# Reordering the start of a sparse-attention and feed-forward kernel: the order of chunk 0's head, and the places of chunk 1's attention steps

## The chip, the cores and the metric

The kernel runs on one NeuronCore of a Trainium2 chip. The core has five engines with queues of their own: TensorE (PE in the profile, with its weight loads as PEld), VectorE (DVE), ScalarE (ACT), GpSimd (POOL) and SyncE (SP, which here only issues DMAs). Each engine takes its instructions strictly in the order of the program, and engines meet through semaphores. The metric is the time of one execution on the device in microseconds, as the median of several runs; less is better.

## The reference

Attention over local and block-summary keys, followed by a gated two-layer network. Four batches, eight heads, 768 positions, head size 64; the network goes from 512 to 2048 and back.

```python
block, window = (32, 16)
k_sum = k.reshape(B, H, nb, block, D).max(axis=3)      # 24 summary keys
v_sum = v.reshape(B, H, nb, block, D).mean(axis=3)     # 24 summary values
scores_l = scale * q @ k.T ; masked where |i - j| >= window
scores_s = scale * q @ k_sum.T + log(block)
a = softmax(concat(scores_l, scores_s))
x = (a @ concat(v, v_sum))            # -> (3072, 512), heads side by side
h = x @ w_in
g = h * sigmoid(beta * h)
out = g @ w_out
```

Inputs and the output are float32; the kernel computes its matmuls in bfloat16.

## The kernel before

**Chunks.** A batch (768 rows of x) is a chunk; four chunks follow each other. A chunk has two parts on PE: the *h stage* (x times w_in, `h_tile`, `h_two`, `h_half`, with silu on ScalarE into `h_sb`) and the *o stage* (h times w_out, `o_mm`, in 24 "atoms" of four matmuls, four atoms to a block of 128 output rows; each block is copied to `o_sb` and stored by SP). The attention of chunk n+1 is spread over the stages of chunk n: `run(main, sides)` writes main step i and then every side step whose position is below i+1. So a position such as 4.5 means "after atom 4". Chunk 0 has nothing to hide behind: its attention is the *head*, written out by hand from line 565 on.

**Attention of a chunk.** The eight heads are four pairs g; a pair's two heads lie on the two halves of the 128 partitions.
- Keys: `kt0(g, bg, cp, km)` turns the loaded rows on PE into PSUM tile big[bg] (`turned`, L260), and `cp` copies them to kT[g] (ScalarE by `act_cp`, VectorE by `dve_cp`). `key_max_nat` (L237) takes block maxima into km[g]. Later chunks: `kt1` or transposing DMAs into kT, `windows_perm` to kw, `key_max_win` (L233), and `key_sums` on GpSimd (L241).
- Queries: `qt_pe` turns pair g in the head, `qt1` all pairs in chunk 1 (L276); copies go to qn[g].
- Scores: `scores0(g, u, bg)` (head) and `scores(b, g, u, bg)` compute half u of pair g into big[bg]; `weigh` takes the exponential on ScalarE (L335). In the head, half u=1 of pairs 2 and 3 is masked by VectorE later (`mask_e`, L339, with the tile `mask`); the other blocks of the head add `off` and `edge` on PE instead. In later chunks all are masked.
- Values: `load_v0`/`load_v` bring float32 values (`vst`), `v_cast` (L344) makes bfloat16 `ve`, `v_odd` (L351, L352) or two DMAs (`v_odd_dma`, L355, L356) make `vo`, the same shifted by 64 rows. Block sums: `vm0`, `vm0s` or `vm_all` on PE, copied to `vm_one` or `vm_sb`; `vm_rest` and `spread` put them into ve and vo.
- AV: `av0` (first half, `av_split`), `av_two` and `av_mm`; `norm` divides on VectorE (L440, L441) into `xn`.
- x turned: `x_pe` and `x_two` on PE in the head, `x_dma` later: a transposing DMA issued by ScalarE (L466) into xT, which the h stage reads.

PSUM has three double tiles big0 to big2 and two single ones, one0 and one1, which everything shares; a step that writes one waits for whoever still reads it.

**Loads.** GpSimd issues keys and queries of chunks 0 and 1 and the weights, w_in in four pieces, then w_out, chunk 1's keys, the rest of w_out and chunk 1's queries (`more_loads`). The first w_in load is held by `behind` until one exponential of the head is done. SP issues the values (those of chunk 1 wait for the last w_out piece), the `vo` DMAs, the stores of the output and, from chunk 2 on, keys (`key_load`, into `kst`) and queries. `blank_run(n)` puts n matmuls on zeros into PE's queue.

**Places of chunk 1's attention.** They stand at lines 704 to 723, over the 24 atoms of chunk 0's o stage: queries at 2.5, value casts at 2.88 to 3.55, scores at 4.5, 9 and 12, block sums at 9, AV at 12.12 for pair 0 and 16.1 to 16.3 for the others, and the loads of chunk 2's keys at 6.5.

Of the kernel before, what the change touches and what calls it, by code (L numbers as in the profile page):

```python
# [11 lines left out]
def kernel(  # L12
# [163 lines left out]
    select(band[:], 2 * W - 1, [[1, QT]], -1)  # L176
    select(As, -W, [[P, J6 + 1], [-block, nb]], 1)
    select(As, block - 1 + W, [[-P, J6 + 1], [block, nb]], -1)

    def more_masks():  # L180
        nc.vector.tensor_copy(out=mask[:], in_=band[:, None, :].to_broadcast([P, NT, QT]))
        nc.vector.memset(mask[0:W, 0], 0.0)
        nc.vector.memset(mask[NK:NK + nb], 1.0)

    def clear_kw():
        for g in range(G):
# [49 lines left out]
    def key_max_nat(g):  # L236
        nc.vector.tensor_reduce(out=km[g][:, NK:NK + nb], in_=kT[g][:, W:W + S].rearrange("p (n f) -> p n f", f=block),  # L237
                                op=ALU.max, axis=AX.X)
# [323 lines left out]
    def blank_run(n, w=P):  # L562
        warm(n, one[1][:, 0, 0:w])

    blank_run(30)
    load_beta()
    blank_run(32, QT)
    kt0(0, 0, act_cp)
    more_masks()
    blank_run(12, QT)  # L570
    kt0(1, 1, act_cp, False)
    blank_run(8)
    kt0(2, 2, dve_cp, False)
    key_max_nat(1)
    blank_run(10)
    kt0(3, 0, act_cp, False)
    blank_run(4)
    v_cast(nc.gpsimd, 0)
    v_odd(nc.gpsimd, 0, 0, 3)
    v_odd(nc.gpsimd, 0, 3, 6)  # L580
    select(mask[0:NK, NT - 1], QT + W - 1, [[0, QT]], -1)

    def av0(g, t):
        av_split(g, t[:, 0])
        norm(0, g, t, [0])

    qt_pe(0, 0, 1, act_cp)
    vm0(0, one[0], dve_cp)
    blank_run(9)
    vm_rest(nc.gpsimd, 0)  # L590
    qt_pe(0, 1, 2, dve_cp)
    scores0(0, 0, 0)
    scores0(1, 0, 1)
    key_max_nat(2)
    key_max_nat(3)
    we = scores0(0, 1, 2)
    av0(0, one[1])
    scores0(1, 1, 0)
    qt_pe(0, 2, 1, dve_cp)
    behind(load_w_in(0, 512), we)  # L600
    v_cast(nc.gpsimd, 1)
    x_pe(0, 0, 0, dve_cp, one[0])
    qt_pe(0, 3, 2, act_cp)
    scores0(2, 0, 0)
    v_odd(nc.gpsimd, 1, 0, 3)
    v_cast(nc.vector, 2)
    v_odd(nc.vector, 2, 0, 3)
    scores0(3, 0, 1)
    scores0(2, 1, 2, False)
    vm0s(1, 2, one[1], dve_cp)  # L610
    scores0(3, 1, 0, False)
    load_w_in(512, 1024)
    v_cast(nc.gpsimd, 3)
    av0(1, one[0])
    av_two(0, 1, [big[2][:, 0:1]])
    v_odd(nc.gpsimd, 3, 0, 3)
    vm0(3, big[1][:, 1:2], dve_cp)
    av0(2, one[1])
    x_pe(0, 1, 0, act_cp, one[0])
    av0(3, big[1][:, 0:1])  # L620
    load_w_in(1024, 1536)
    load_w_in(1536, 2048)

    def begin(p, lo, hi):
        for i in (2 * p, 2 * p + 1):
            h_begin(i, big[(2, 0, 1)[p % 3]][:, i % 2], lo, hi)

    begin(0, 0, 1)
    begin(1, 0, 1)
    x_pe(0, 2, 0, act_cp, one[1])  # L630
    silu_table()
    begin(0, 1, 2)
    begin(1, 1, 2)
# [44 lines left out]
    HB = [one[1], big[1], one[0]]  # L678
    run([lambda i=i: h_half(i, 1, HB[i % 3][:, 0]) for i in range(k2)], s)

    def load_keys(n):
        for g in range(G):
            key_load(n, g)


    def av_at(b, s, pos, bufs):
        for g in range(G):
            def av(g=g):
# [8 lines left out]
    def x_pe2(b, g, t):  # L697
        t = t.bitcast(bf16)[:, 0, 0:S]
        x = xn[(b, g)]
        for j in range(J6):  # L700
# [10 lines left out]
    for j, (g, u, bg, pos, late) in enumerate([(0, 0, 2, 4.5, 4.6), (0, 1, 1, 4.5, 4.61), (1, 0, 0, 4.5, 4.62), (1, 1, 2, 9, 9.2),  # L711
                                               (2, 0, 1, 9, 9.11), (2, 1, 0, 9, 9.12), (3, 0, 2, 12, 12.13), (3, 1, 1, 12, 12.14)]):
# [12 lines left out]

# [82 lines left out]
```

## Time and profile before

| what | us |
|---|---|
| three runs | 214.63, 215.19, 217.09 (median 215.19) |
| the profiled execution | 216.31, of which the span from first to last instruction is 214.5 |
| head: PE's first h matmul (L495) | starts at 24.31 |
| chunk 0's first o matmul (L527) | starts at 48.95 |
| chunk 1's first scores (L328) | start at 55.36, after 0.35 of waiting |
| chunk 1's block sums (L388) | start at 60.41 |
| chunk 1's first h matmuls (L509) | two at 76.08, the rest from 77.78 |
| chunks 2 and 3: h stage starts | 123.55 and 169.48 |

The granted TensorE clock is full (1.000) over the whole span. The page's 40 slices show where each engine and the DMA engines are busy, in tenths, 5.4 us to a slice:

```profile
PE   7989999999999979999999999999999999999993
PEld 7877666665445446665555466654555566654452
DVE  5497757299657723950798325744787200002121
ACT  2468595686767007778633046778450086650000
POOL 7938980002701103563003004444000000000000
PEclk9999999999999999999999999999999999999999
DMA  6999999999669999999689879999535500001212
```

A busy slice of PE need not be useful work: in the head, 105 of its matmuls are blanks. VectorE's row shows the two crowded stretches, slices 2 and 3 (5 to 11 us: 4 and 9) and slices 8 to 10 (43 to 59 us). The DMA row is at nine or more until 54 us: weights, keys, queries and values of chunk 1 come in one unbroken stream.

The transposing DMAs into xT before chunk 1's h stage took 4.9 to 6.8 us from issue to landing; over all twelve in the run the median is 4.0.

### The profile page before, as it was taken

Reading aid. Unit: us, or ns where it says so; the run is one execution under the profiler, and the core shown is the slowest. Engines: PE = TensorE matmul, PEld = TensorE weight load, DVE = VectorE, ACT = ScalarE, POOL = GpSimd, SP = SyncE. Lnnn points to the kernel's source line nnn. Section 1 sums busy time; section 2 is a strip of 40 time slices with the busy share of each in tenths; the row PEclk is TensorE's granted clock in tenths of the full one; section 3 lists DMA queues with packets and bytes.
Section 4 is the critical chain, followed back from the end, with each engine's and each line's share of the span. In section 5 each row is a group of like instructions: output and inputs, shape, how many; then the busy total and the mean of one; then the engine's idle time right before and its main releaser. Section 6 shows DMA issues by size and latency. Waiting matters only on the chain.

```text
span 214.5 us, 5288 instructions
## 1 busy us (share of the span) xinstructions
PE 205.0 (96%) x2225; PEld 122.0 (57%) x2242; DVE 109.4 (51%) x252; ACT 106.5 (50%) x140; POOL 54.2 (25%) x85
## 2 busy tenths in 40 slices
PE   7989999999999979999999999999999999999993
PEld 7877666665445446665555466654555566654452
DVE  5497757299657723950798325744787200002121
ACT  2468595686767007778633046778450086650000
POOL 7938980002701103563003004444000000000000
PEclk9999999999999999999999999999999999999999
DMA  6999999999669999999689879999535500001212
GB/s 122 197 224 170 192 180 206 206 207 216 132 191 229 222 239 228 221 201 167 135 256 229 188 167 232 165 206 201 133 124 111 151 11 0 0 3 49 98 49 98
DMA packets 74534, 34.08 MB, mean 159 GB/s; under 512 B 61440, under 2 KB 70032, under 8 KB 74512
## 3 DMA queue, kind: packets, MB, share of 16 engines
q1 hardware_dynamic: 57440, 24.05, 53.0%
q0 software_dynamic: 7440, 7.34, 21.4%
q10 hardware_dynamic: 9632, 2.37, 8.0%
q8 instruction: 17, 0.28, 0.6%
q14 instruction: 5, 0.04, 0.1%
HBM read 27.37 MB, written 6.29 MB: 157 GB/s over the span
## 4 chain that ended last, share of the span: by engine, by line
PE 82%; DVE 12%; DMA 3%; issue 2%; ACT 0%; DVEq 0%
PE one L527 34%; PE big L509 29%; PE big L495 5%; DMA xT<-xn 3%; DVE kw L247 2%; PE big L328 2%; PE one L544 2%; PE big L414 2%; DVE qn L247 2%; DVE km L233 2%; DVE w_out_sb L216 2%; DVE xn L441 1%; PE one L501 1%; DVE km L237 1%; PE big L315 1%
## 5 line engine op out<-in xcount | busy, mean ns | idle before, releaser
L527 PE MATMUL one<-w_out_sb,h_sb 128*128 128x512 bf16 (+1 forms) x383 | 83.4, 370 | 1.9 <-issue 1.4
L522 ACT ACTIVATE h_sb<-big,beta_sb 128x768 bf16<-128x768 f32 x48 | 42.7, 900 | 49.1 <-PE big L509 49.1
L509 PE MATMUL big<-xT,w_in_sb 128*128 128x384 bf16 x384 | 63.1, 326 | 1.2 <-DMA xT<-xn 1.2
L527 PEld LDWEIGHTS <-h_sb 128*128 128x128 bf16 x400 | 38.1, 98 | 41.3 <-issue 0.2
L509 PEld LDWEIGHTS <-w_in_sb 128*128 128x128 bf16 x384 | 37.6, 98 | 26.5 <-issue 1.4
L247 DVE COPY o_sb<-one 128x512 f32<-128x512 f32 x19 | 13.1, 690 | 45.1 <-PE one L527 44.9
L335 ACT ACTIVATE e<-big,bias 128x768 bf16<-128x768 f32 x32 | 26.7, 897 | 16.5 <-PE big L328 13.9
L339 DVE TENSOR_TENSOR e<-e,mask 128x768 bf16<-128x768 bf16 x26 | 14.3, 571 | 15.8 <-ACT e L335 15.7
L247 DVE COPY kw<-kT 128x960 bf16<-128x960 bf16 (+1 forms) x16 | 10.5, 696 | 15.1 <-DMA kT<-kn 14.9
L344 POOL CAST ve<-vst 128x832 bf16<-128x832 f32 x15 | 13.7, 926 | 6.9 <-DMA vst<-in_v_dram 3.8
L475 POOL CAST qn<-qst 128x768 bf16<-128x768 f32 x8 | 6.6, 826 | 32.7 <-DMA qst<-in_q_dram 32.7
L241 POOL COPY kw<-km 128x288 bf16<-128x288 bf16 x12 | 7.5, 633 | 26.6 <-DVE km L233 26.6
L441 DVE TENSOR_TENSOR xn<-big,r 128x768 bf16<-128x768 f32 (+1 forms) x14 | 12.6, 900 | 0.5
L495 PE MATMUL big<-xT,w_in_sb 128*128 128x384 bf16 x64 | 11.4, 326 | 0.0
L233 DVE TENSOR_REDUCE km<-kw 128x24 bf16<-128x768 bf16 x12 | 11.2, 946 | 0.2
L483 POOL CAST kn<-kst 96x1024 bf16<-96x1024 f32 x4 | 4.1, 1037 | 23.3 <-DVE e L339 22.8
L642 ACT ACTIVATE h_sb<-big,beta_sb 128x384 bf16<-128x384 f32 x16 | 8.1, 579 | 2.7 <-PE big L495 2.7
L544 PE MATMUL one<-blank 128*128 128x128 bf16 (+1 forms) x105 | 8.2, 249 | 1.3 <-DVE blank L125 1.3
L501 PEld LDWEIGHTS <-w_in_sb 128*128 128x128 bf16 x64 | 6.2, 98 | 4.1
L501 PE MATMUL one<-xT,w_in_sb 128*128 128x384 bf16 x44 | 8.1, 326 | 0.0
L544 PEld LDWEIGHTS <-blank 128*128 128x128 bf16 x105 | 7.0, 121 | 1.7 <-DVE blank L125 1.3
L495 PEld LDWEIGHTS <-w_in_sb 128*128 128x128 bf16 x64 | 5.9, 98 | 3.5
(126 smaller groups left out, 186.9 us busy)
## 6 DMA issues: line engine op xcount, KB each, us to landing
out_dram<-o_sb SPq DMA_DIRECT2D x23, 256.0 KB, 2.7
vst<-in_v_dram SPq DMA_DIRECT2D x13, 336.0 KB, 4.5
kst<-in_k_dram SPq DMA_DIRECT2D x8, 384.0 KB, 5.9
qst<-in_q_dram SPq DMA_DIRECT2D x8, 384.0 KB, 4.2
w_in_sb<-in_moe_w_in_dram POOLq DMA_DIRECT2D x4, 512.0 KB, 6.3
w_out_sb<-in_moe_w_out_dram POOLq DMA_DIRECT2D x4, 512.0 KB, 13.6
vo<-ve SPq DMA_DIRECT2D x12, 107.2 KB, 2.3
vst<-in_v_dram SPq DMA_DIRECT2D x3, 416.0 KB, 7.1
```

What stands on the lines that cost most here:

```text
L233: nc.vector.tensor_reduce(out=km[g][:, NK:NK + nb].rearrange("p (m n) -> p m n", n=2), in_=kw[g][:, :, W:W + QT].rearrange("p m (n f) -> p ...
L247: nc.vector.tensor_copy(out=o, in_=i)
L335: return nc.scalar.activation(out=e[:], in_=s[:, :, 0:HS], func=ACTF.Exp, bias=bias[:, 0:1], scale=scale)
L339: return nc.vector.tensor_mul(out=e.rearrange("p h (m q) -> p h m q", q=QT), in0=e.rearrange("p h (m q) -> p h m q", q=QT), in1=mask[:, No ...
L344: eng.tensor_copy(out=ve[:, g, lo:hi, 0:D], in_=vst[g][:, lo:hi])
L441: nc.vector.tensor_mul(out=x[:, 3 * us[0]:3 * us[0] + 3 * n].rearrange("p (k j) h d -> p k (j h) d", k=n), in0=tv[:, :, :, 0:D], in1=r[:, ...
L495: nc.tensor.matmul(t[:, 0:HS], w_in_sb[:, ki, i * P:(i + 1) * P], xT[:, ki, 0:HS], start=(ki == 0), stop=(ki == k1 - 1))
L501: nc.tensor.matmul(t[:, 0:HS], w_in_sb[:, ki, i * P:(i + 1) * P], xT[:, ki, lo:lo + HS], start=(ki == 0), stop=(ki == k1 - 1))
L509: nc.tensor.matmul(t[:, kk, 0:HS], w_in_sb[:, ki, i * P:(i + 1) * P], xT[:, ki, kk * HS:(kk + 1) * HS], start=(ki == 0), stop=(ki == k1 - 1))
L522: nc.scalar.activation(out=h_sb[:, i, :].rearrange("p (k m) -> p k m", k=2), in_=t[:, :, 0:HS], func=ACTF.Silu, scale=beta_sb[:, i:i + 1])
L527: nc.tensor.matmul(t[:, 0:hi - lo], h_sb[:, n, ms * P:(ms + 1) * P], w_out_sb[:, n, lo:hi], start=(n == 0), stop=(n == k2 - 1))
L544: nc.tensor.matmul(t, blank[:, 0:P], blank[:, 0:t.shape[-1]], start=True, stop=True)
```

## The change

Four things are rearranged; no arithmetic changes, and outside the head and chunk 1's attention nothing is touched.

- *Head, keys and masks.* The function `more_masks` (fill the whole `mask` tile from `band`, 128 partitions) is dropped. A memset of the summary rows (partitions 96 to 127) stands early, and the copy of the other 96 partitions, its small memset and GpSimd's select on the last tile come much later. Pair 1's block maxima follow its key copy at once; pair 3's keys are copied by VectorE instead of ScalarE. Four blank matmuls go, and nine become seven.
- *Head, order of pairs.* Both score halves of pair 0 come before pair 1's queries are turned, AV of pair 0's first half before pair 1's scores. The first w_in load is held behind pair 1's first exponential instead of pair 0's second (each the third that ScalarE takes). Pair 3's queries are turned ahead of x of pair 0.
- *Head, values.* Pair 2's cast goes from VectorE to GpSimd, right behind pair 1's; pair 1's odd part goes from GpSimd to VectorE. Block sums of pairs 1 and 2 come after all scores. AV of pair 3 and the turn of pair 2's x come ahead of the first h matmuls; pair 3's block sums are copied by ScalarE.
- *Chunk 1.* Scores, block sums, AV, x DMAs and table loads from atom 8 on are placed one atom earlier. The block maxima of pair 3 go from position 0.4 to 3.44, behind the query copies. Two of chunk 2's four key loads go from 6.5 to 2.896, the others to 3.56.

```diff
-    def more_masks():
-        nc.vector.tensor_copy(out=mask[:], in_=band[:, None, :].to_broadcast([P, NT, QT]))
-        nc.vector.memset(mask[0:W, 0], 0.0)
-        nc.vector.memset(mask[NK:NK + nb], 1.0)
...
     load_beta()
+    nc.vector.memset(mask[NK:P], 1.0)
     blank_run(32, QT)
     kt0(0, 0, act_cp)
-    more_masks()
     blank_run(12, QT)
-    kt0(1, 1, act_cp, False)
+    kt0(1, 1, act_cp)
     blank_run(8)
     kt0(2, 2, dve_cp, False)
-    key_max_nat(1)
     blank_run(10)
-    kt0(3, 0, act_cp, False)
-    blank_run(4)
+    kt0(3, 0, dve_cp, False)
...
-    select(mask[0:NK, NT - 1], QT + W - 1, [[0, QT]], -1)
...
     vm0(0, one[0], dve_cp)
-    blank_run(9)
     vm_rest(nc.gpsimd, 0)
-    qt_pe(0, 1, 2, dve_cp)
-    scores0(0, 0, 0)
-    scores0(1, 0, 1)
+    blank_run(7)
+    scores0(0, 0, 2)
     key_max_nat(2)
+    scores0(0, 1, 0)
+    qt_pe(0, 1, 1, dve_cp)
+    av0(0, one[1])
     key_max_nat(3)
-    we = scores0(0, 1, 2)
-    av0(0, one[1])
+    we = scores0(1, 0, 2)
+    behind(load_w_in(0, 512), we)
+    v_cast(nc.gpsimd, 1)
     scores0(1, 1, 0)
     qt_pe(0, 2, 1, dve_cp)
-    behind(load_w_in(0, 512), we)
-    v_cast(nc.gpsimd, 1)
+    qt_pe(0, 3, 2, act_cp)
     x_pe(0, 0, 0, dve_cp, one[0])
-    qt_pe(0, 3, 2, act_cp)
+    nc.vector.tensor_copy(out=mask[0:NK], in_=band[0:NK, None, :].to_broadcast([NK, NT, QT]))
+    nc.vector.memset(mask[0:W, 0], 0.0)
+    v_odd(nc.vector, 1, 0, 3)
+    v_cast(nc.gpsimd, 2)
     scores0(2, 0, 0)
-    v_odd(nc.gpsimd, 1, 0, 3)
-    v_cast(nc.vector, 2)
-    v_odd(nc.vector, 2, 0, 3)
     scores0(3, 0, 1)
     scores0(2, 1, 2, False)
-    vm0s(1, 2, one[1], dve_cp)
     scores0(3, 1, 0, False)
+    v_odd(nc.vector, 2, 0, 3)
     load_w_in(512, 1024)
     v_cast(nc.gpsimd, 3)
-    av0(1, one[0])
-    av_two(0, 1, [big[2][:, 0:1]])
     v_odd(nc.gpsimd, 3, 0, 3)
-    vm0(3, big[1][:, 1:2], dve_cp)
+    vm0s(1, 2, one[1], dve_cp)
+    av_two(0, 1, [one[0]])
+    av0(1, big[1][:, 0:1])
     av0(2, one[1])
-    x_pe(0, 1, 0, act_cp, one[0])
-    av0(3, big[1][:, 0:1])
     load_w_in(1024, 1536)
     load_w_in(1536, 2048)
+    select(mask[0:NK, NT - 1], QT + W - 1, [[0, QT]], -1)
+    vm0(3, big[2][:, 0:1], act_cp)
+    x_pe(0, 1, 0, act_cp, one[0])
...
+    av0(3, big[1][:, 0:1])
+    x_pe(0, 2, 0, act_cp, one[1])
     begin(0, 0, 1)
     begin(1, 0, 1)
-    x_pe(0, 2, 0, act_cp, one[1])
...
-         (.3, lambda: km_pe(2, nc.gpsimd)), (.4, lambda: km_pe(3, nc.gpsimd))]
+         (.3, lambda: km_pe(2, nc.gpsimd)), (3.44, lambda: km_pe(3, nc.gpsimd))]
...
-  (0, 0, 2, 4.5, 4.6), (0, 1, 1, 4.5, 4.61), (1, 0, 0, 4.5, 4.62), (1, 1, 2, 9, 9.2),
-  (2, 0, 1, 9, 9.11), (2, 1, 0, 9, 9.12), (3, 0, 2, 12, 12.13), (3, 1, 1, 12, 12.14)
+  (0, 0, 2, 4.5, 4.6), (0, 1, 1, 4.5, 4.61), (1, 0, 0, 4.5, 4.62), (1, 1, 2, 8, 8.2),
+  (2, 0, 1, 8, 8.21), (2, 1, 0, 8, 8.22), (3, 0, 2, 11, 11.13), (3, 1, 1, 11, 11.14)
...
-    s.append((12.09, silu_table))
-    s.append((9.0, lambda: vm_all(one[1], [dve_cp] * 4)))
-    s.append((9.05, lambda: spread(0)))
-    s.append((9.06, lambda: spread(1)))
-    av_at(1, s, [12.12, 16.1, 16.2, 16.3], [0, 1, 2, 0])
+    s.append((11.09, silu_table))
+    s.append((8.0, lambda: vm_all(one[1], [dve_cp] * 4)))
+    s.append((8.1, lambda: spread(0)))
+    s.append((8.11, lambda: spread(1)))
+    av_at(1, s, [11.12, 15.1, 15.2, 15.3], [0, 1, 2, 0])
     for g in range(G):
-        s.append(((12.2, 16.35, 16.4, 16.5)[g], lambda g=g: x_dma(1, g)))
-    s.append((6.5, lambda: load_keys(2)))
+        s.append(((11.2, 15.35, 15.4, 15.5)[g], lambda g=g: x_dma(1, g)))
+    for g in range(G):
+        s.append(((2.896, 2.897, 3.56, 3.561)[g], lambda g=g: key_load(2, g)))
```

More of the change, by code (lines that the diff above doesn't have):

```diff
@@ L679 @@
     run([lambda i=i: h_half(i, 1, HB[i % 3][:, 0]) for i in range(k2)], s)
-    def load_keys(n):
-        for g in range(G):
-            key_load(n, g)
     def av_at(b, s, pos, bufs):
@@ L710 @@
         s.append(((2.885, 2.895, 3.45, 3.55)[g], lambda g=g: v_odd_dma(g)))
-    for j, (g, u, bg, pos, late) in enumerate([(0, 0, 2, 4.5, 4.6), (0, 1, 1, 4.5, 4.61), (1, 0, 0, 4.5, 4.62), (1, 1, 2, 9, 9.2),
-                                               (2, 0, 1, 9, 9.11), (2, 1, 0, 9, 9.12), (3, 0, 2, 12, 12.13), (3, 1, 1, 12, 12.14)]):
+    for j, (g, u, bg, pos, late) in enumerate([(0, 0, 2, 4.5, 4.6), (0, 1, 1, 4.5, 4.61), (1, 0, 0, 4.5, 4.62), (1, 1, 2, 8, 8.2),
+                                               (2, 0, 1, 8, 8.21), (2, 1, 0, 8, 8.22), (3, 0, 2, 11, 11.13), (3, 1, 1, 11, 11.14)]):
         s.append((pos + .01 * j, lambda g=g, u=u, bg=bg: scores(1, g, u, bg)))
         s.append((late, lambda g=g, u=u: last_mask.update({1: mask_e(1, g, u)})))
-    s.append((12.09, silu_table))
-    s.append((9.0, lambda: vm_all(one[1], [dve_cp] * 4)))
-    s.append((9.05, lambda: spread(0)))
-    s.append((9.06, lambda: spread(1)))
-    av_at(1, s, [12.12, 16.1, 16.2, 16.3], [0, 1, 2, 0])
+    s.append((11.09, silu_table))
[3 more added lines that the diff above has]
+    av_at(1, s, [11.12, 15.1, 15.2, 15.3], [0, 1, 2, 0])
     for g in range(G):
-        s.append(((12.2, 16.35, 16.4, 16.5)[g], lambda g=g: x_dma(1, g)))
-    s.append((6.5, lambda: load_keys(2)))
+        s.append(((11.2, 15.35, 15.4, 15.5)[g], lambda g=g: x_dma(1, g)))
+    for g in range(G):
+        s.append(((2.896, 2.897, 3.56, 3.561)[g], lambda g=g: key_load(2, g)))
     run(main, s)
```

## The prediction

> **What bounds the kernel now.** I read the page's busy times first, then the chain of waits in order of time, then the list of waits, and last each engine's timeline from 0 to 82 us.
>
> ```profile
> PE 205.0 (96%) x2225; PEld 122.0 (57%) x2242; DVE 109.4 (51%) x252; ACT 106.5 (50%) x140; POOL 54.2 (25%) x85
> ```
>
> PE is busy for 205.0 of 214.5 us, so 9.5 us are open. The chain says where they lie; its columns are start, length, what.
>
> ```profile
> 7.95 0.95 DVE km L237
> 8.90 0.67 DVE mask L181
> 9.57 0.05 issue
> 9.62 0.09 DVE mask L182
> 9.71 0.20 issue
> 9.91 0.70 DVE mask L183
> 10.60 0.03 issue
> 10.63 0.96 DVE kT L247
> 11.59 0.86 DVE km L237
> 12.45 0.03 issue
> 12.48 0.30 DVE vm_one L247
> 12.78 0.03 issue
> 12.81 0.97 DVE qn L247
> ...
> 53.48 1.74 DVE qn L247 x2
> 55.22 0.14 issue
> ...
> 72.30 5.44 DMA xT<-xn
> 77.74 0.04 issue
> 77.78 20.64 PE big L509 x126
> ```
>
> The list of waits has what PE lost at these places (total, times, longest, in us):
>
> ```profile
> PE big L509 <- DMA xT<-xn: 1.2, 1, 1.2
> ...
> PE big L307 <- DVE qn L247: 1.0, 2, 0.6
> ...
> PE big L328 <- DVE qn L247: 0.3, 1, 0.3
> ```
>
> So three stretches set the end. In the head (to 24.3 us) VectorE's queue does; PE's "busy" there is mostly blank matmuls. At 55.2 PE waits for VectorE's query copies, at 77.8 for a transposing DMA. From 24.3 to 55 and from 77.8 to the end PE runs without a gap worth naming: an instant won on PE before those stretches is won at the end, if transfers keep up.
>
> **The change, part by part. Head.** I follow each engine's order after the change with the durations of before. ScalarE's first two kT copies end at 7.95 and 8.83 as now. VectorE: km0 7.95 to 8.90; the mask work of 1.70 us (8.90 to 10.60) leaves this place; km1 to 9.80 (0.9); kT2 to 10.75 (0.96); kT3, new here (ScalarE had it, 10.17 to 10.97), +0.9 to 11.65; vm_one +0.3 to 12.0; km2 +0.95 to 12.95. The memset that remains (0.70 for 24 partitions, now 32) starts near 5.35, where VectorE idles 2.59 us; uncovered it would cost those 0.70.
>
> PE: four blanks (0.33 us) go, so pair 0's query turn starts at 10.06 instead of 10.39. Its load is no bar: the value load ordered behind it issued at 9.91. ScalarE, rid of kT3, copies qn0 10.63 to 11.43 (0.80). Block sums of pair 0 10.52 to 11.02, seven blanks (0.067 each) to 11.49: covered by that copy. Pair 0's scores 11.50 and 12.11 (0.61 each), first exponential 12.32 (0.82 after its scores start, as now) to 13.22; now it starts at 13.24. Pair 1's query turn 12.74 to 13.20, then its copy on VectorE, 13.31 to 14.27, which is 0.5 later than now (12.81); under it PE does pair 0's AV (0.60) to 13.87 and waits 0.44. Pair 1's scores 14.31 to 15.53, where now the fourth scores block ends at 16.5. VectorE meanwhile normalises (0.2 and 0.56) and does km3, to 15.85. Query turn of pair 2 15.55; pair 3's needs exponential 3 (15.13 to 16.03), 16.07 to 16.53. qn2 on VectorE 16.12 to 17.08 (now 17.11 to 18.07), qn3 on ScalarE to 17.65. Pair 2's scores start at 17.12 instead of 18.12; the four exponentials end at 21.2 instead of 22.2.
>
> The tail. VectorE takes xT0 to 17.35, the mask copy (0.67) and memset to 18.1, both halves of the odd values of pair 1 (0.25 each) to 18.65, of pair 2 to 19.5: it would idle there (0.67 before vm_one now). GpSimd: the first w_in load waits for exponential 3, as now for the third one: issue 16.33 (now 16.63); casts of pairs 1 and 2 to 18.95 (0.88 each), w_in to 19.7, cast 3 to 20.6, its odd part to 21.7, two w_in loads to 23.3, the select to 23.55; then nothing has moved (its next copy started at 23.62). PE: block sums of pairs 1 and 2 at 19.30; AV of pair 0's second half 19.8; AV 1 at 20.25 after vm_one; AV 2 20.9; block sums 3 21.5 to 22.0, copied by ScalarE to 22.4 (bounded by 0.30 on VectorE's row and 0.48 on ScalarE's xT row; 0.3 taken, the nearer shape); AV 3 22.47 to 23.1; turn of pair 2 to 23.27; four h matmuls each (0.65) to 24.57. Here pair 3's turn starts, which now starts at 25.79 with the same work behind it: **1.22 us**. Bounds: qn1 could be 0.3 earlier, km3 or a cast 0.4 later, so 0.8 to 1.5.
>
> Do loads keep up? First w_in chunk lands 5.6 after 16.63, 22.2, need 23.27. The second lands at 25.8, need 26.05; the third at 28.3, need 28.7. Keys of chunk 1 land at 38.2 (27.6 plus 10.6), need 38.90; queries at 50.1 (30.59 plus 19.5), need 50.41. All hold, narrowly, with nothing issued later than now.
>
> **First chunk.** km3 (0.86) goes behind the two query copies. PE's turns end at 51.96 with the head's shift, so the copies run 52.0 to 53.74 and the scores start at 53.88 instead of 55.36: 1.48, of which 1.22 is the head's: **0.26**. The third wait (0.35) falls to 0.1. km3 now follows at 54.6 and its GpSimd copy (0.43) sits ahead of the last value cast; that cast waits for data until 56.8 anyway, so this costs nothing; if data came early, 0.43 on the cast.
>
> All scores, block sums and AV one atom sooner (4 matmuls, 0.87 us): PE's work is the same, only its order changes, so nothing is won on PE itself. AV of pairs 1 to 3, the normalisations and the transposes start 0.87 sooner against the h stage, whose wait is 1.21: **0.87**, up to 1.21 if the transposes land faster. ScalarE's output copy of row block 2 (0.59) now stands right before the last two exponentials, whose row starts 0.2 behind PE: 0.3 later, covered by VectorE's idle 1.08 before the normalisation at 69.41.
>
> Two key loads (384 KB each, 0.45 to 0.59 of SP's queue) move ahead of the first output store and the odd-value transfers of pairs 2 and 3. Waiting behind them on SP: vo2, vo3 (before 59.21 and 60.49, landing 2.1 later), and for those VectorE's spreading of pairs 2 and 3, at 64.00 now, 61.65 after. vo3 issues at 59.4 to 60.4 and lands 2.1 to 3.2 later (the two rows of vo landings, alone and beside value loads): 61.5 to 63.6, a wait of 0 to 1.9 against the idle 1.08. I take 0. In return the transposes no longer share engines with key loads that took 4.1 to 7.5 us from 61.65: they landed in 4.9 to 6.8 us here, 4.0 in the median of all twelve. That is up to 0.34 more; I take 0.05.
>
> Sum: 1.22 + 0.26 + 0.87 + 0.05 = 2.4 us. The profiled execution took 216.31 us (span 214.5 and 1.8 around it), so 213.9; it lies 1.12 above the median of the three runs, and from that median, 215.19, the time is **212.8 us**.
>
> **The rivals.** (a) *Value casts late, 15%.* PE now reaches chunk 1's block sums at 58.06 (60.41 less 1.48 and 0.87). The last cast ended at 57.98 after a wait for its load. Now vo0 and vo1 can go 0.9 sooner, beside that load; beside loads vo1 took 3.2 us against 2.1. If the load loses those 0.9, PE stands 0.9: gain 1.5, 213.7.
>
> (b) *Mask copy against a GpSimd cast, 7%.* The mask copy (17.35) would fall on the cast of pair 1 (17.14 to 18.0). If one had to wait for the other, casts end 0.67 later: block sums of pairs 1 and 2 0.35 later, and everything that GpSimd issues behind slips 0.67, which leaves the last cast of chunk 1 0.2 short: gain 1.85, 213.3. Against it: the copy ran at 8.81 for 0.75 us beside the cast at 8.47, which took 0.88, as the undisturbed one at 55.57. For it: the cast at 56.82 took 1.16 beside a mask multiply. [...]
>
> (c) *The key loads stand in the way, 10%, and slower 4%.* Between 46 and 58 us SP's issues took up to 2.07 each (the 48 KB value parts) and 1.71 (vo1). If the two key loads cost that, vo3 lands by 66 and the spreading waits 4.4, of which 3.3 reach the transposes. It decides from a wait of 1.08; from 3.4 the change is slower than before, at 4.4 by 0.9: 216.1; a third such issue makes it over 1%, 218.2. Against: four key loads in a row took 2.07 in all. At the mild end, 0.7 over the slack, 213.5. [...]
>
> (d) *The head's gain does not arrive, 8%*: a link of the long head chain is later than reckoned, or queries of chunk 1 (0.3 us of room) come late. Only the atom and the query copies remain: gain 1.2, 214.0.
>
> **The numbers.** Forecast 56%, its own range 212.2 to 213.2. Over 1% (2.15 us, about what a measurement of this kernel can tell from no change) faster means below 213.04: most of the forecast (0.48) and the good ends of the rivals (0.06), 0.54. Slower by over 1% 0.04, mostly (c). Within 1% 0.42. Low end: all of 2.69 (1.48 and 1.21) and the lowest run's 0.56 below the median, 211.9; high end: (d) with 0.4 of scatter, 214.4. The claim that PE's later work is rigid carries most.
>
> **What would show it.** Mask work gone from 8.9 and vm_one near 12.0; first exponential near 12.3; pair 2's scores near 17.1; pair 3's turn near 24.6; chunk 1's scores near 53.9; the h stage of chunk 1 starting near 75.4. Wrong: PE waits for a weight load or for ve before 60 us, VectorE waits for vo at 61.7, or the transposes' wait at 1.2 as now.

## The result and the profile after

The change made the kernel slower: 218.38 us in the median of 6 runs (217.07 to 220.07) against 215.08 (214.63 to 217.09), a ratio of 1.0144 with a 95% interval of 1.0104 to 1.0183. (Medians here and below are of all runs; ratios are of the means, without runs over 1.5% above the kernel's fastest.) The profiled execution after the change took 219.03 us with a span of 217.1. Line numbers shift between kernels: L242 after is L247 before.

The page after the change, first its busy times and then, from the 40 slices, the granted clock (a 9 is full speed; each slice is 5.4 us):

```profile
PE 209.2 (96%) x2236; PEld 123.2 (57%) x2236; DVE 112.2 (52%) x253; ACT 105.9 (49%) x140; POOL 53.5 (25%) x84
...
PEclk9999679999999999999999999999999999999999
```

PE is 4.2 us busier than in the profile before (205.0) for the same work, and two slices, from 21.7 to 32.6 us, have a lower clock. The same stretch in windows of 2 us; behind the engines' busy times stand the clock, the DMA share and GB/s:

```profile
20.00:22.00 2.00, 0.65 (x25) 0.43 (x18) 1.97 (x3) 1.57 (x2) 1.90 (x4) 1.00 1.24 201
22.00:24.00 2.00, 1.62 (x37) 1.34 (x38) 1.84 (x7) 0.00 (x0) 1.88 (x4) 0.72 1.24 201
24.00:26.00 2.00, 2.00 (x28) 1.64 (x28) 0.81 (x3) 0.74 (x2) 1.77 (x5) 0.50 1.21 193
26.00:28.00 2.00, 2.00 (x15) 1.08 (x12) 0.75 (x2) 1.36 (x2) 1.94 (x4) 0.50 1.24 206
28.00:30.00 2.00, 2.00 (x11) 1.18 (x10) 0.39 (x2) 0.61 (x2) 2.00 (x4) 0.57 1.20 178
30.00:32.00 2.00, 2.00 (x14) 1.22 (x13) 1.97 (x7) 1.33 (x3) 1.51 (x2) 1.00 1.19 186
```

TensorE, the first figure, works 0.65 us of the first window. Then its clock is at half for 6.8 us, and eight h matmuls take 2.77 us, where they take 1.46 at full clock (in the six-blanks kernel below, at 26.24). In windows of 0.5 us the low clock begins at 22.9 and ends at 29.7. The list of waits names the idle time in the first row, and the other places that the prediction looked at:

```profile
PE big L417 <- DVE vm_one L242: 1.7, 1, 1.7
...
DVE ve L394 <- DMA vo<-ve: 1.4, 1, 1.4
...
PE big L302 <- DVE qn L242: 0.9, 2, 0.5
```

PE's wait for the transposes (1.2 before) is gone from the list, and the chain of waits reaches the h stage of chunk 1 later all the same:

```profile
56.73 1.83 DVE qn L242 x2
58.56 0.14 issue
58.69 0.70 PE big L323 x36
...
76.19 5.56 DMA xT<-xn
```

Scores of chunk 1 start at 58.69 instead of 55.36. So the loss lies ahead of them. PE's wait is for the averages of pairs 1 and 2, and what VectorE does ahead of those is in its timeline:

```profile
17.59 0.87 DVE L596 COPY mask<-band 96x768 bf16<-96x768 bf16 x1
18.52 0.09 DVE L597 MEMSET mask<- 16x32 uint32 x1
18.62 0.69 DVE L346 COPY vo<-ve 64x384 bf16<-64x384 bf16 x1
19.33 1.57 DVE L347 COPY vo<-ve 32x384 bf16<-32x384 bf16 x1
20.92 0.54 DVE L346 COPY vo<-ve 64x384 bf16<-64x384 bf16 x1
21.48 0.53 DVE L347 COPY vo<-ve 32x384 bf16<-32x384 bf16 x1
22.04 0.60 DVE L242 CAST vm_one<-one 32x128 bf16<-32x128 f32 x2
```

GpSimd's timeline for the same stretch:

```profile
17.38 1.83 POOL L339 CAST ve<-vst 128x832 bf16<-128x832 f32 x2
19.15 0.74 POOL L205 DMA_DIRECT2D w_in_sb<-in_moe_w_in_dram  x1
19.89 0.89 POOL L339 CAST ve<-vst 128x832 bf16<-128x832 f32 x1
20.84 0.50 POOL L346 COPY vo<-ve 64x384 bf16<-64x384 bf16 x1
21.39 0.50 POOL L347 COPY vo<-ve 32x384 bf16<-32x384 bf16 x1
```

The four odd copies take 3.33 us, where the prediction had 1.0. Each ends 0.10 to 0.12 us after a GpSimd instruction does: 19.31 behind the casts' 19.21, 20.90 behind 20.78, 21.46 behind 21.34, 22.01 behind 21.89. The averages are done 2 us later than forecast, PE idles 1.73 us, and the clock falls.

Two theories were put against each other at first. *A*: the copies beside GpSimd delay PE, the idle time drops the clock, and the rest of the change works as forecast. Its rivals: the clock falls for the new order itself, or the loss comes from chunk 1. All were tested with the kernel before beside every batch (medians of 215.40 to 215.54 there).

### The profile page after: what moved, and what is told of

The parts are those of the page before. It is cut to its first block, busy times and chain, and to the rows that moved or that the text cites. A ratio compares the mean times of both kernels' runs of the same rounds, so it can differ in the third digit from the quotient of the medians.

```text
span 217.1 us, 5292 instructions
## 1 busy us (share of the span) xinstructions
PE 209.2 (96%) x2236; PEld 123.2 (57%) x2236; DVE 112.2 (52%) x253; ACT 105.9 (49%) x140; POOL 53.5 (25%) x84
## 3 DMA queue, kind: packets, MB, share of 16 engines
q1 hardware_dynamic: 57440, 24.05, 52.9%
## 4 chain that ended last, share of the span: by engine, by line
PE 87%; DMA 5%; DVE 4%; POOL 1%; issue 1%; POOLq 0%; DVEq 0%
PE one L522 36%; PE big L504 28%; PE big L490 6%; PE one L496 3%; DMA xT<-xn 3%; PE big L409 3%; PE big L323 2%; DMA qrow<-in_q_dram 2%; DVE qn L242 2%; PE big L496 1%; PE big L271 1%; DVE vo L347 1%; PE one L383 1%; POOL krow L87 1%; PE big L255 1%
## 5 line engine op out<-in xcount | busy, mean ns | idle before, releaser
L522 PE MATMUL one<-w_out_sb,h_sb 128*128 128x512 bf16 (+1 forms) x400 | 85.8, 371 | 0.0
L504 PE MATMUL big<-xT,w_in_sb 128*128 128x384 bf16 x384 | 63.0, 326 | 0.1
L504 PEld LDWEIGHTS <-w_in_sb 128*128 128x128 bf16 x384 | 37.6, 98 | 25.4 <-issue 0.3
L242 DVE COPY o_sb<-one 128x512 f32<-128x512 f32 x19 | 13.1, 689 | 45.8 <-PE one L522 45.7
L334 DVE TENSOR_TENSOR e<-e,mask 128x768 bf16<-128x768 bf16 x26 | 14.8, 592 | 13.3 <-ACT e L330 13.2
L242 DVE COPY kw<-kT 128x960 bf16<-128x960 bf16 (+1 forms) x16 | 10.5, 702 | 15.2 <-DMA kT<-kn 15.1
L490 PE MATMUL big<-xT,w_in_sb 128*128 128x384 bf16 x64 | 12.8, 356 | 0.0
L490 PEld LDWEIGHTS <-w_in_sb 128*128 128x128 bf16 x64 | 6.6, 107 | 4.3 <-issue 1.2
L539 PE MATMUL one<-blank 128*128 128x128 bf16 (+1 forms) x99 | 7.4, 246 | 1.3 <-DVE blank L125 1.3
L496 PEld LDWEIGHTS <-w_in_sb 128*128 128x128 bf16 x64 | 6.2, 98 | 4.1
L498 ACT ACTIVATE h_sb<-one,beta_sb 128x384 bf16<-128x384 f32 x11 | 6.4, 580 | 2.2 <-PE one L496 1.7
```

Source lines behind the costliest of these rows:

```text
L242: nc.vector.tensor_copy(out=o, in_=i)
L334: return nc.vector.tensor_mul(out=e.rearrange("p h (m q) -> p h m q", q=QT), in0=e.rearrange("p h (m q) -> p h m q", q=QT), in1=mask[:, No ...
L490: nc.tensor.matmul(t[:, 0:HS], w_in_sb[:, ki, i * P:(i + 1) * P], xT[:, ki, 0:HS], start=(ki == 0), stop=(ki == k1 - 1))
L496: nc.tensor.matmul(t[:, 0:HS], w_in_sb[:, ki, i * P:(i + 1) * P], xT[:, ki, lo:lo + HS], start=(ki == 0), stop=(ki == k1 - 1))
L504: nc.tensor.matmul(t[:, kk, 0:HS], w_in_sb[:, ki, i * P:(i + 1) * P], xT[:, ki, kk * HS:(kk + 1) * HS], start=(ki == 0), stop=(ki == k1 - 1))
L522: nc.tensor.matmul(t[:, 0:hi - lo], h_sb[:, n, ms * P:(ms + 1) * P], w_out_sb[:, n, lo:hi], start=(n == 0), stop=(n == k2 - 1))
```

## Experiments on the clock

**The head alone**: the head of after with the first chunk of before.

> The head of the change alone, chunk 1's places as before. Theory A: the whole loss is here: clock 0.98 to 0.99, time 219.4 us (218 to 221), and the difference to the whole change is what the chunk 1 part wins (about 1.1). Rival D: the loss is in the chunk 1 part, and this runs at 214.

Measured 218.55 us (217.47 to 219.62, 4 runs), ratio 1.0144 (1.0089 to 1.0199). All 4 runs had a clock of 0.984 to 0.991. In the profiled one PE idled 1.19 us before 22.00. So the head alone is as slow as the whole change, and the chunk part does not win the 1.1 us that was expected of it.

**Blanks in the hole**, in the kernel after; `warm(n, tile)` puts n blank matmuls into PE's queue:

```diff
     av_two(0, 1, [one[0]])
+    warm(26, big[1][:, 0, 0:P])
```

> The changed kernel with 26 blank matmuls put into PE's queue ahead of pair 1's AV, where PE now stands idle for 1.73 us (20.6 to 22.4); nothing else differs. Theory A: VectorE's odd-value copies are held up by GpSimd, so vm_one is late, PE stands idle, and the idle stretch makes the chip grant PE half its clock for two stretches of 3.4 us (22.9 to 29.7), which costs most of the loss. Then the mean clock is 1.000, VectorE's copies are as late as now (vm_one near 22.0), pair 3's x turn comes near 27 instead of 28.9, and the time is 215.2 us (214.6 to 215.8), ratio to the kernel before near 1.00. Rival B: the half clock has another cause (the eleven or so blanks taken out of the head before 12 us): then it stays at 0.98 to 0.99 and the time at 217 to 219. Rival C: the clock is an accompaniment and the wait itself costs all: 218.

216.77 us (215.92 to 220.01), ratio 1.0051 (1.0026 to 1.0075). The averages are as late as in after (rival B's "eleven or so" missing blanks are six, 105 against 99 on the two pages); PE's row in the timeline shows the blanks and no more than 0.18 us of waiting, and the clock stays at 1.00 in 9 of 10 runs:

```profile
20.34 1.63 PE L539 MATMUL big<-blank 128*128 128x128 bf16 x26
22.15 0.34 PE L417 MATMUL big<-vm_one,e 128*128 128x65 bf16 x6 [0.18 <-DVE vm_one L242]
```

Work without a use wins 1.6 us (218.38 to 216.77), with the averages as late as ever: so much at least was the clock's part. But the result is 1.3 above the kernel before, not level with it as expected, so something else is left to explain.

**A delay in the order of before**: four memsets of a scratch tile on VectorE ahead of the averages. **The same with 26 blanks.** And, later, **two memsets more**.

```diff
+    for n in range(3):          # 5 in the longer one
+        nc.vector.memset(idle_t[:], 0.0)
+    nc.vector.memset(idle_t[:, 0:384], 0.0)
     vm0s(1, 2, one[1], dve_cp)
     scores0(3, 1, 0, False)
```

> The kernel before with four extra memsets on VectorE (2.5 us) ahead of the averages of pairs 1 and 2, nothing else: TensorE idles there. The memsets replace 0.67 us of idle time, so the averages come 1.8 us later and TensorE idles about 1.7 us, as in the kernel after. Theory A (such an idle stretch halves the granted clock for one or two stretches of 3.4 us, whatever the order): clock 0.984 to 0.992, time 1.7 plus 1.7 to 3.4 over the kernel before, 218.6 to 220.5, ratio 1.015 to 1.024. Rival G (the clock fell for something else in the changed head): clock 1.000, 217.0, ratio 1.007.

> The eleventh run with 26 blank matmuls (1.63 us) in the stretch where TensorE would idle: the same delay without the idle time. Theory A: clock 1.000, time 1.6 to 1.9 over the kernel before, 216.9 to 217.4, ratio 1.007 to 1.009, and 1.7 to 3.4 us under the eleventh run. Rival G: as the eleventh run.

> The eleventh run with two more memsets on VectorE (0.96 us), so that TensorE idles 2.6 us in the order of the kernel before. Theory W: the work in the grid stretch falls from 0.29 to about 0.2, the clock is 0.984 to 0.992 in most executions, time 0.96 plus 1.7 to 3.4 over the eleventh run's 216.38: 219.0 to 220.8. Theory A as first held (idle time alone, whatever the order) says the same here. Rival G (only the changed head drops the clock): clock 1.000 in most executions, 217.3.

The delay: 216.38 us (215.81 to 218.25), ratio 1.005 (1.0025 to 1.0074). A miss: PE waited as long as in after, and the clock stayed up in 10 of 12 runs.

```profile
20.21 0.42 PE L316 MATMUL big<-qn,kT 64*96 64x64 bf16 x12
...
22.31 0.35 PE L423 MATMUL one<-vm_one,e 128*128 128x65 bf16 x6 [1.68 <-DVE vm_one L248]
```

With blanks 216.92 (216.23 to 219.0), 1.007 (1.0038 to 1.0103), no clock under 0.995 in 10 runs: no gain, since there was no drop to prevent. The longer delay: 219.1 us (217.07 to 220.24), 1.0155 (1.0116 to 1.0194), a drop in 5 of 6 runs. So the new order is not needed for the drop, and the length of the idle time alone does not decide it: 1.19 us was enough in the head alone, 1.68 mostly not here.

What parts them shows in where the clock changes. Read in windows of 0.5 us, the low stretch of after is 22.89 to 29.72, that of the head alone 24.23 to 27.65: 6.83 and 3.42 us, two times and one time 3.41. After PE has stopped at the end of the program the clock falls once more, at 217.45 and 215.38: 194.56 and 191.15 us after the first drops, which is 57 steps and 56 steps of 3.413 us. So in these two profiles the falls of the clock and the rise between them lie on a grid of that step, which starts at 2.41 us in the one and at 0.34 in the other. The other profiles show the fall at the end alone (before: 214.62), and I took their grid from it; that they have one is an estimate from the two. I then worked out, for the grid stretch that holds the idle time, the work of the array: columns of all matmuls in it, each times the share of the 128x128 array that it uses, over the 8,192 columns of 16 w_out matmuls (16 of 512; they take 3.56 us at full clock in the profile of after, so that a stretch full of them comes to 0.96). The measure and its yardstick are mine; that the array could do no more in 3.41 us is not shown. The figures are good to about 0.02; a run counts as one with a drop where its mean clock is 0.992 or less.

| kernel | PE's wait, us | work in its grid stretch | runs with a drop |
|---|---|---|---|
| after | 1.73 | 0.24 | 6 of 6 |
| head alone | 1.19 | 0.26 | 4 of 4 |
| longer delay | 1.82 | 0.28 (this execution kept the clock) | 5 of 6 |
| delay | 1.68 | 0.29 | 2 of 12 |
| delay and blanks | 0.89 | 0.30 | 0 of 10 |
| values back (below) | 0.83 | 0.32 | 1 of 10 |
| before | 0.23 | 0.41 | 0 of 110 |

**Six blanks in the hole** was the test of that: little work added, most of the idle time left.

```diff
     av_two(0, 1, [one[0]])
+    warm(6, big[1][:, 0, 0:P])
```

> The kernel after with 6 blank matmuls of 128x128 (0.38 us) where TensorE idles 1.73 us, against the 26 of the first run. Theory W (the work of one grid stretch decides: matmul columns, weighted by the share of the 128x128 array that each uses, over what the array could do in 3.41 us; worked out from the profiles it was 0.24 in the kernel after and 0.26 in the head alone, which dropped the clock, and 0.29, 0.30, 0.30 and 0.32 in the eleventh, ninth, twelfth and second run, which did not): the blanks add 0.09, so 0.33 and clock 1.000 in most executions, though 1.3 us of idle time stay; time 216.4 to 217.0, as the first run. Rival L (the length of the idle stretch decides, and 1.19 us was enough in the head alone): clock 0.984 to 0.992 as in the kernel after, 217.1 to 219.2.

216.75 us (215.44 to 218.47), ratio 1.0052 (1.0021 to 1.0083). PE still waited 1.29 us, more than in the head alone, and 7 of 12 runs kept the clock (median 215.94), 5 lost one stretch (217.53). That is between the two expectations. In its profiled execution, which kept the clock, a line of the grid (23.03) falls into the hole, and the stretches on its two sides hold about 0.4 each. All this fits a threshold on the work of a grid stretch, near 0.26 to 0.28, with the grid lying differently in each run; that it is this measure of work, and not another that falls and rises with it, is not shown, since only the profiled executions could be laid on their grid. PE's idle time, counted within the grid stretch, parts them nearly as well: 1.73 and 1.25 us in the two that dropped, 1.30, 1.19, 1.10 and 0.83 in the four below them that did not.

One stretch costs 1.6 us here (217.53 less 215.94). In after the three runs with one stretch (mean clocks of 0.990 to 0.992) have a median of 217.43, the three with two (0.983 and 0.984) 219.17: 1.74 more. Taking 1.74 off the 217.43 leaves 215.7, some 0.6 above the kernel before; by this estimate 2.7 of the 3.3 us lost are the clock's. The kernel with 26 blanks, at 216.77, gives 1.6. What makes up the 1.1 between the two is open.

## Experiments on VectorE's copies

**Values back**: the odd copies of pair 1 on GpSimd and the cast of pair 2 on VectorE, as before the change.

```diff
-    v_odd(nc.vector, 1, 0, 3)
-    v_cast(nc.gpsimd, 2)
+    v_odd(nc.gpsimd, 1, 0, 3)
+    v_cast(nc.vector, 2)
```

> The changed kernel with pair 1's odd values on GpSimd and pair 2's cast on VectorE again, as in the kernel before; everything else of the change stays, the fewer blanks too. Theory A: the odd copies of pair 1 and 2 no longer run beside GpSimd's casts on VectorE (0.25 each instead of 0.5 to 1.6), vm_one near 20.4, PE waits 0.3 at most there, clock 1.000, pair 3's turn near 25, time 213.2 us (212.7 to 213.8). Rival B (fewer blanks): clock still below 0.995, time over 216. Rival D (the key loads ahead of the odd values lose what the rest wins): clock 1.000, but no better than 215.

216.19 us (214.99 to 218.63), ratio 1.003 (1.0004 to 1.0057); clock 1.000 in the profile. VectorE's two odd copies took 0.57 and 0.97 beside GpSimd, and PE still waited 0.83. Theory A missed by 3 us; rival D's two figures (clock 1.000, no better than 215) came out, its cause is taken up with the key loads below.

**GpSimd held**: its next load of w_in, and the cast of pair 3 behind that, wait for VectorE's last odd copy.

```diff
-    v_odd(nc.vector, 2, 0, 3)
-    load_w_in(512, 1024)
+    od = v_odd(nc.vector, 2, 0, 3)
+    behind(load_w_in(512, 1024), od)
```

> The kernel after, but GpSimd's next transfer of w_in, and with it the cast and the odd copies of pair 3's values behind it, start only when VectorE has done the odd copies of pair 2. Theory A (the odd copies of VectorE are slow because GpSimd works beside them, that delays the averages, TensorE idles 1.7 us, and the granted clock falls to half): first odd copy about 0.7 still, beside GpSimd's cast of pair 2; the next three 0.25 each; averages of pairs 1 and 2 at 20.2 to 20.5 instead of 22.04; TensorE's wait for them under 0.3 us; clock 1.000; pair 3's x turn 25.0 to 25.6; time 214.5 to 215.3, ratio 0.996 to 1.001. Rival B (the copies are slow for another reason, or the clock falls for the changed order itself): odd copies 0.5 to 1.6 again or clock 0.984, time 217 to 218.5.

VectorE's timeline there:

```profile
18.65 0.69 DVE L346 COPY vo<-ve 64x384 bf16<-64x384 bf16 x1
19.35 0.25 DVE L347 COPY vo<-ve 32x384 bf16<-32x384 bf16 x1
19.62 0.26 DVE L346 COPY vo<-ve 64x384 bf16<-64x384 bf16 x1
19.89 0.25 DVE L347 COPY vo<-ve 32x384 bf16<-32x384 bf16 x1
20.41 0.60 DVE L242 CAST vm_one<-one 32x128 bf16<-32x128 f32 x2 [0.27 <-PE one L367]
```

The first copy still ends with GpSimd's cast (19.23); the next three, with GpSimd waiting, take a quarter of a microsecond each. The averages come at 20.41, and 11 of 12 runs kept the clock. This settles the odd copies: it was GpSimd that held them (1.57, 0.54 and 0.53 in after against 0.25, 0.26 and 0.25). Yet the kernel takes 216.63 us (216.23 to 219.07), ratio 1.0061 (1.0032 to 1.009), above the expected 214.5 to 215.3 and no better than with the blanks. Some 0.6 of it is the experiment's own: from pair 3's turn of x to the first w_out matmul it takes 23.74 us, where the other kernels that kept the clock take 23.15 or 23.16, and 0.4 of that is a wait of PE for the held w_in loads.

**Mask late**: values back, and the mask copy with its memset and GpSimd's select moved behind the last AV of the head.

> The kernel after with the values split as before (odd copies of pair 1 on GpSimd, cast of pair 2 on VectorE, as in the second run of this study) and with VectorE's mask copy and its memset moved behind the averages, to after the last AV of the head. Theory A: VectorE's row ahead of the averages of pairs 1 and 2 is 0.97 us shorter than in that run, the odd copies meet the end of GpSimd's row as before and take 0.25 to 0.6 each, averages at 20.2 to 20.6 (21.26 there), TensorE waits under 0.3 us for them (0.83 there), clock 1.000, pair 3's x turn 25.0 to 25.5; time 0.6 to 0.9 us under that run's 216.19: 215.3 to 215.6, ratio 0.999 to 1.001. Rival B (VectorE's row is not what TensorE waited for): 216.0 to 216.4.

The averages came at 20.76, no wait of PE for them is left over 0.15 us, and no run lost the clock. But 216.76 us (215.54 to 217.66), ratio 1.0065 (1.0038 to 1.0091): the expected 0.6 to 0.9 did not come. Both kernels lose in chunk 1, as the next section shows.

**The mask copy was held as well.** In its late place, with GpSimd idle, the copy of 96 partitions took 0.35 us, against 0.87 in after. The kernel before has the same copy, with 128 partitions, beside a cast on GpSimd; in the longer delay, whose head is that of before up to there, it starts 0.02 us ahead of the cast instead of 0.34 behind:

```profile
8.81 0.75 DVE L181 COPY mask<-band 128x768 bf16<-128x768 bf16 x1
8.47 0.88 POOL L344 CAST ve<-vst 128x832 bf16<-128x832 f32 x1
...
8.49 0.35 DVE L182 COPY mask<-band 128x768 bf16<-128x768 bf16 x1
8.51 1.07 POOL L345 CAST ve<-vst 128x832 bf16<-128x832 f32 x1
```

In before (the first two lines) the copy takes 0.75 and ends 0.21 us behind the cast, as it does in after behind the first of two casts (18.46 against 18.25). In the longer delay the copy takes 0.35, and it is the cast that takes 1.07 instead of 0.88. So in these two pairs the one that started second took longer, the copy by 0.40 us and the cast by 0.19.

## Experiments on the first chunk

**The chunk part alone**, on the head of before, was the first sign:

> The kernel before with the chunk 1 part of the change alone (atom earlier, key maxima of pair 3 and key loads moved). Theory A: clock 1.000, chunk 1's scores wait less and the wait for the transposes at the start of chunk 1's h stage falls from 1.2 to under 0.4: 214.0 us (213.7 to 214.4), ratio 0.995. Rival D: 215 or more, with VectorE waiting for the odd-value DMAs for over 1.1 us.

216.09 us (214.73 to 216.84), ratio 1.0021 (0.9996 to 1.0047), where 214.0 was expected. **The kernel before once more** says why nothing was won:

> The kernel before, unchanged, a second time: it shows how far two profiled executions of one kernel lie apart, and whether the wait of 1.21 us of TensorE for the transposes in the h stage of chunk 1 (at 77.78 in the first profile), which the chunk part was to remove, is there in every execution. Theory C, the wait was a feature of one execution (the first profile's execution took 216.31 us, about 1 us over the median of the kernel's runs): a wait under 0.5 us there, profiled span 213 to 213.6. Rival D, the wait is always there, and the chunk part does remove it but pays for it elsewhere: a wait of 1.0 to 1.4 again. Ratio by both 0.997 to 1.003.

215.2 us (214.33 to 216.35), ratio 0.999 (0.9964 to 1.0016), profiled span 213.2. PE's timeline of this second profile at the h stage:

```profile
74.70 1.46 PE L527 MATMUL one<-w_out_sb,h_sb 128*128 128x512 bf16 x6
76.00 21.09 PE L509 MATMUL big<-xT,w_in_sb 128*128 128x384 bf16 x128
```

No wait for the transposes. The 1.21 us that the chunk part was to win was there in the one execution that was first profiled (216.31 us, about 1 over the median), and not in this one, which took 215.12 us, as the median. Theory C holds for these two. The other kernels above that have chunk 1 as before agree: PE waited 0.5 us for transposes in the head alone and in the delay with blanks, and not at all in the two delays without. In five of these six profiles there is 0.5 us or nothing to remove.

What earlier block sums can cost shows in the kernels whose head is not late. With GpSimd held in the head, GpSimd's timeline is this:

```profile
55.26 0.88 POOL L339 CAST ve<-vst 128x832 bf16<-128x832 f32 x1 [0.17 <-DMA vst<-in_v_dram]
57.83 1.15 POOL L339 CAST ve<-vst 128x832 bf16<-128x832 f32 x1 [1.69 <-DMA vst<-in_v_dram]
58.93 0.75 POOL L236 COPY kw<-km 128x288 bf16<-128x288 bf16 x1
60.32 0.88 POOL L339 CAST ve<-vst 128x832 bf16<-128x832 f32 x1 [0.65 <-DMA vst<-in_v_dram]
```

And PE's:

```profile
59.75 0.24 PE L383 MATMUL one<-ve,A_avg 128*32 128x128 bf16 x3
61.25 0.56 PE L383 MATMUL one<-ve,A_avg 128*32 128x128 bf16 x25 [1.26 <-POOL ve L339]
```

GpSimd waits for the value loads three times, 2.5 us in all, and PE, an atom sooner at the block sums, waits for the last cast: 1.26 us here, 1.82 with the mask late, 0.34 with values back. In after there is no such wait; there PE comes to the block sums 3 us later.

**Key loads back** to atom 6.5: on the kernel before with the rest of the chunk part, and on the mask-late kernel. **The mended head** (that of mask late) **without the chunk part** parts the two halves.

> The kernel before with the chunk part, but all four key loads at atom 6.5, where they were. Theory C (the chunk part has nothing to remove in most executions, TensorE is the bound there): as the chunk part alone, 216.1 less or more 0.5, ratio 1.000 to 1.003. Rival D (the key loads on SP ahead of the odd values of pairs 2 and 3 cost about what the earlier block sums gain): 0.8 to 1.2 us under the chunk part alone, 214.6 to 215.2, ratio 0.995 to 0.999; no wait of the spread for the odd values.

> The seventh run (changed head with values split as before and mask copy late, and the chunk part) with all key loads back at atom 6.5. If the early key loads cost what parts the third run (216.1) from the eighth (215.2): 0.7 to 1.0 under the seventh run's 216.76, 215.8 to 216.1, the wait of the spread for odd values gone. If the early block sums against late value casts are the whole loss: the wait at the block sums of 1.2 to 1.8 again, 216.5 to 217.0.

> The head of the seventh run (the changed head with the values split as before and the mask copy behind the last AV) and the chunk part undone. Theory A' (with the clock held and VectorE's row short, the changed head is worth nothing: the first profile of that head starts its w_out matmuls at 49.00 where the kernel before has 48.95 and 48.86; and what the seventh run lost, 1.3 us, it lost in chunk 1, where the block sums waited 1.82 us for GpSimd's value casts): first w_out matmul 48.8 to 49.2, wait for the casts at the block sums of chunk 1 under 0.3, time 215.0 to 215.5, ratio 0.998 to 1.001. Rival E (the head itself is slower, by landings that come later): 216.2 to 216.8 as the seventh run. Rival F (the head's forecast gain is there once the chunk part is out): 214.0 to 214.4.

On the head of before: 215.21 us (214.64 to 219.26), ratio 0.9982 (0.996 to 1.0004), the time of its rival D. On the mended head: 216.6 (216.09 to 219.11), 1.0051 (1.0023 to 1.0078), with the wait for the casts (1.26) again, as its second theory has it. The mended head alone: 215.82 (214.75 to 218.36), 1.0013 (0.9987 to 1.0039), between A' and E. VectorE's wait for odd values, 0.9 to 1.8 us in every profile with the early key loads, is gone in these three. Where PE stands, from its timelines:

| kernel | first w_out matmul, chunk 0 | the same, chunk 1 | between | wait for casts |
|---|---|---|---|---|
| before, second profile | 48.86 | 96.92 | 48.06 | none |
| keys back | 48.93 | 97.29 | 48.36 | 0.39 |
| chunk part alone | 49.87 | 98.08 | 48.21 | none |
| mended head alone | 49.33 | 97.97 | 48.64 | 0.49 |
| mended head, keys back | 48.75 | 97.98 | 49.23 | 1.26 |
| GpSimd held | 49.32 | 98.56 | 49.24 | 1.26 |
| mask late | 49.00 | 99.38 | 50.38 | 1.82 |
| after, blanks | 49.95 | 97.72 | 47.77 | none |
| after | 52.45 | 100.64 | 48.19 | none |

The second column says that the mended head, with GpSimd held too, is level with before (48.75 to 49.33 against 48.86 and 48.95), and the interval of the mended head alone leaves at most 0.3 us of gain: the forecast microsecond was not won. (The chunk part alone is a microsecond late there: in that execution PE waited 1.7 us for the head's key and query loads.) The fourth says that, against the second profile of before, the chunk part wins 0.3 at best (the kernel with blanks, whose values are in time) and loses up to 2.3; the first profile of before, with its wait for the transposes, has 49.3. When the values land differs between executions by itself: SP's first value load of chunk 1 started at 45.83, 46.10, 47.13 and 47.69 in four profiles that are one program up to there. Two things stay open: whether the early key loads cost anything (216.09 against 215.21 on the head of before, 216.76 against 216.60 on the mended one), and why PE's wait for the casts is longer behind the changed head (0.34 to 1.82) than with the chunk part on the head of before (0.39 in the one profile whose head was in time). No kernel of this study beats the one before.

## Why the prediction was wrong

It forecast 212.8 us, the range to 214.4, and gave slower 4%.

- **The step that failed first** is the tail of the head: "both halves of the odd values of pair 1 (0.25 each) to 18.65, of pair 2 to 19.5: it would idle there". The price came from a row of before (0.26 and 0.25 at 19.29) where GpSimd mostly issued a load beside them; the change put GpSimd's casts and copies there. They took 3.33 us in place of 1.0. With GpSimd held three of the four took 0.25, as priced. The prediction had GpSimd's new row in the same paragraph, cast by cast, and laid it beside the mask copy only.
- **Rival (b)** was right in kind, and the argument against it misread its row. The prediction took the copy at 8.81 (0.75 us beside a cast) for one that was not held. That copy takes 0.35 in the longer delay, where it started first, so the row speaks for (b), and so does after's 0.87. The copies' ends agree, 0.10 to 0.12 us behind GpSimd's for the odd values and 0.21 for the mask; by what means the two hold each other up no run shows. Only the direction of (b) was off: the casts, which had started first, kept their time (0.88 us in before, 1.83 for the two in after), and the copy waited. Its price of 0.67 for the mask copy was a held one already, so that term came near; (b)'s question, put to the odd copies, would have shown them held.
- **The step that made it large** is "PE's later work is rigid", at a full clock. It held where the clock held (mask late: 23.15 us from pair 3's turn to the first w_out matmul, before 23.16), but for the kernel whose w_in loads were held (23.74). After has 23.51, and most of the clock's cost ahead of that turn. The prediction had no term for a clock that falls: it took PE's later work at full clock throughout.
- **The head's 1.22 us** was mis-sized even so. With GpSimd held pair 3's turn starts at 25.58, against 25.79 and 25.70 in the two profiles of before: 0.1 to 0.2. Of the missing microsecond 0.5 was gone by the block sums (19.79, forecast 19.30), in small steps: 0.08 at pair 0's query turn, 0.27 at pair 1's scores, 0.37 at pair 2's (17.49). The rest came behind the averages, 0.3 of it as a hole inside AV 3 (23.92) that the profile puts to nothing. "Its load is no bar" did not hold either: PE waited 0.25 us for the queries in after and 0.73 in the mended head alone.
- **Right**, or nearly, were the steps up to the tail: in after vm_one is done at 11.61 (forecast 12.0), the first exponential starts at 12.40 (12.32), pair 2's scores at 17.47 (17.12; 18.12 before).
- **The atom's 0.87** was the size of a wait that the second profile of before does not have. The prediction saw that its execution lay 1.12 us over the median and took that off as a constant, when the wait was likely most of it.
- **Rival (a)**, values late at chunk 1's block sums, came true wherever the head was in time, at 0.3 to 1.8 us where the prediction had 0.9. **Rival (c)**'s mild end is there (VectorE waited 1.4 us for odd values) and cost PE nothing that shows. How the key loads slow the odd values is not shown: SP issues both, and the DMA view of before has one queue, q1, whose 24.05 MB are about the sum of all that SP issues. **Rival (d)**, at 214.0, was right that the head's gain does not arrive, and too mild.

## What to carry to other kernels

Price an instruction by a row with the same neighbour on the other engines, and when a change moves work on two engines, lay the new rows side by side for every instruction, above all for copies between SBUF tiles beside GpSimd. A row that seems to refute a theory needs its own undisturbed time beside it: 0.75 us looked free until the same copy took 0.35. Before counting a wait of the profile as a gain, ask whether that execution is the median's: take a second profile. Ahead of a stretch that TensorE bounds, a hole among small matmuls can cost its length again or more through the clock: here one of 1.73 us went with 1.6 to 2.7 us, by the two estimates above. 26 blank matmuls in it prevented that in 9 of 10 runs here, six in 7 of 12.

## What was not expected of the hardware

- The granted clock fell to half for one or two stretches of 3.41 us after idle times of 1.19 and 1.73 us in the two profiles that show it, on a grid that lies differently in the two (its steps start at 0.34 and 2.41 us). In each the fall at the end comes a whole number of steps of 3.413 us behind the first drop, 56 and 57. The length of the idle time alone did not decide: the head alone, with 1.19 us in its profile, lost the clock in 4 of 4 runs (0.984 to 0.991), the delay, with 1.68, in 2 of 12.
- A copy of 32 partitions by 384 bf16 took 1.57 us instead of 0.25 beside GpSimd. Between 19.33 and 19.89 GpSimd only issued a load. Copies in other rows were held beside an issue too, in its later part: in the profile of before a copy at 27.13 took 0.54 and ended 0.06 us behind an issue, while one that was over 0.45 us into an issue, at 19.56, took 0.25. The held copy would have been over 0.43 us into its issue; in the longer delay one with that place (19.62) took 0.25. What decides at this edge is not settled.
- It goes the other way as well: a GpSimd copy that started 0.02 us behind one of VectorE's (19.25, mended head alone) took 0.61 us instead of 0.50.
